# One Trainium2 core, a transformer block: query-key products two feature groups at a time, one evacuation for three modulation rows, a new order of work

## The chip, the cores and the metric

The kernel runs on one core of a Trainium2 chip. The metric is device time in microseconds (us) of one execution. A core has five engines, each with its own queue that it works through in order: TensorE (PE in the profile; PEld is its weight load), VectorE (DVE), ScalarE (ACT), GpSimd (POOL) and SyncE (SP), which here only issues transfers (DMA). SBUF is the on-chip memory of 128 partitions, PSUM the memory that TensorE writes.

## The reference

The block is modulated by a vector `c`: its SiLU, multiplied by `w_mod`, gives six rows of 512 (`sa`, `ca`, `ga`, `sb`, `cb`, `gb`). Part A is attention over 2048 positions with 32 heads of 16 features, in which each query sees 8 keys, at distances 0, 2, ... 14. Part B is a token mixer: an MLP along the positions.

```python
    def _A_ref(x, wqkv, wo):            # H = 32, Dh = 16, W, dil = 8, 2
        ...
        logits = jnp.einsum('bhsd,bhswd->bhsw', q, kg) * scale
        logits = jnp.where(mask[None, None, :, :], logits, -1000000000.0)
        attn = _softmax(logits, axis=-1)
        o = jnp.einsum('bhsw,bhswd->bhsd', attn, vg)
        return (lambda x, *d: x.transpose(*d))(o, 0, 2, 1, 3).reshape(B, S, D) @ wo
    def _B_ref(x, w1, b1, w2, b2):
        h = _layernorm(x, axis=-1)
        u = _gelu(jnp.einsum('bsd,sf->bdf', h, w1) + b1)
        y = jnp.einsum('bdf,fs->bds', u, w2) + b2
        return (lambda x, *d: x.transpose(*d))(y, 0, 2, 1)
    ...
    h = _layernorm(x, axis=-1) * (1 + ca) + sa
    x = x + ga * _A_ref(h, A_wqkv, A_wo)
    h = _layernorm(x, axis=-1) * (1 + cb) + sb
    x = x + gb * _B_ref(h, B_w1, B_b1, B_w2, B_b2)
```

## The kernel before

The 2048 positions are 16 tiles of 128. They go through part A in five chunks of 2, 4, 4, 4 and 2 tiles (`SIZES`), so a chunk has C = 256 or 512 columns. Part B follows once the second layernorm of the tiles it needs is done.

**Order.** The program is a graph of some 780 named operations. `ORDER` (from line 192) is a table of their names, written out in full, that sets the place of each in its engine's queue; a letter behind the name picks the engine where there are several (`:a` ACT, `:d` DVE, `:p` POOL, `:s` SP), `:q` asks for a TensorE product in four pieces of 32 output partitions, `:n` leaves an accumulation into PSUM to the evacuating engine, and `fill:n` puts n idle products on TensorE. `schedule` (line 86) walks the table and hands out buffers of three rings: six PSUM tiles (`ps`), four product buffers (`big`) and five value buffers (`vd`). Nearly all instructions are recorded by one helper, so they carry line 143; they are told apart by tiles and shapes.

**Part A of chunk c, by the names of the table.** `ln1s`, `ln1v`, `rstd1`, `nb1` are the statistics of the first layernorm and `n1_t` its output for tile t. `xt` transposes two tiles by DMA (chunks 2 to 4; `tr` does it on TensorE for 0 and 1). `qkv{c}_{t}{j}` multiplies by the weights (t = 0 query, 1 key, 2 value; j the feature group), and `ev{c}_{t}{j}` evacuates the result. The 16 features of a head are held as 4 groups of 4, so `qk{c}_{d}` (line 761) multiplies, for group d, the queries with the 8 shifted keys: 8 x C products a partition into one `big` buffer. `red{c}_{d}` sums four partitions of it on TensorE into the PSUM tile `psL`, over the four groups. Then come `max` (DVE, from `psL`), `sub` (TensorE), `exp` (ACT), `esum` (TensorE; DVE in chunk 4), `rcp` (ACT) and `smB` (DVE), whose result `lsb` is spread over partitions by four transfers `a2_{c}_{j}`. Four transfers `vd{c}_{q}` bring shifted values, `pv{c}_{q}` (DVE) multiplies them with the weights into a `big` buffer, `pvacc` (TensorE) sums, `oev` (ACT) evacuates, `wo{t}` (TensorE) multiplies by `wo`, and `x1_{t}` adds into `xx`.

**Second layernorm and part B.** `ln2q`, `rstd2`, `nb2`, `n2_t` (layernorm), `aff` (line 903: times 1 + cb, plus sb, on a group of tiles), `ln3s`, `ln3v`, `rstd3`, `nb3`, `h3_t` (part B's own layernorm). `mlp1_{i}_{f}_{s}` is the first product for feature tile f and position tiles from s on; it comes in two or three sweeps i, whose partial sums `park` and `padd` keep in `gT`. The pieces whose names end in `_10` with i = 1 and f from 7 on need all of `h3` from tile 10 to 15. Then `gelu`, `mlp2` for each of 16 output tiles, `fin` (two DVE operations) and the store `st_out`.

**Modulation rows.** `build_mod_rows` (line 588) makes four rows: `modrow0` (ga), and `modrow1` (sb, cb, gb together) on TensorE; `mrows0` on ACT and `mrows1` on DVE bring them to SBUF. `mrows1` is two DVE instructions, a copy of three rows, and a second read of the middle one with 1 added. `st_row` and `ld_row` then spread the rows over all partitions through DRAM.

`halo_k3` copies the last 16 key columns of chunk 2 to the start of the key buffer that chunk 3 reuses; it may run only when chunk 2's `qk` are done.

Of the kernel before, what the change touches and what calls it, by code (L numbers as in the profile page):

```python
# [8 lines left out]
ALU = mybir.AluOpType  # L9
# [33 lines left out]
class _Graph:  # L43
# [42 lines left out]
    def schedule(self):  # L86
# [4 lines left out]
        for pos, token in enumerate(ORDER.split()):  # L91
# [111 lines left out]
wsc1_1:p wsc0_2:p n1_7:p n1_9:p wsc1_2:p n1_6:p smB0 qk1_2 wsc2_3:a qkv1_22:q red1_0 qkv1_21:q modrow1 wsc2_0:a
a2_0_1:a ev1_22:a ev1_21:a ln1s15 nb1_3 red1_1 qkv1_23:q red1_2 red1_3 mrows1 max1 xt6 xt8 qkv1_20:q ev1_23:a wsc2_1:a
ev1_20:a qkv2_00:q qkv2_10:q vd0_2 vd0_3 vd0_1 ld_wo2 vd0_0 st_row0 a2_0_2:s a2_0_3:s a2_0_0:s ld_wo3 ld_row0 ld_wo0
n1_11:p n1_10:p pv0_1 pv0_2 pv0_3 pv0_0 sub1:q ev2_00:a biascols_cp:a exp1 ev2_10:a qkv2_03:q pvacc0_2 qkv2_11:q
fill:6:q qkv2_13:q esum1:q pvacc0_3 n1_12:a n1_13:a ev2_13:a ev2_03:a oev0_2:a pvacc0_0 pvacc0_1 rcp1 rstd1_4 oev0_0:a
qk2_0 woq_s smB1 qk2_3 qkv2_01:q qkv2_12:q qkv2_02:q ev2_11:a ev2_01:a a2_1_1:a ev2_12:a ev2_02:a qk2_1 qk2_2 wo1:q
x1_1:a wo0:q x1_0:a ln2q1 xt10 xt12 red2_0 qkv2_23:q qkv3_22:q qkv3_12:q vd1_0 st_row1 vd1_2 ev2_23:a ln2q0 rstd2_0
nb1_4 nb2_0 qkv2_21:q ev2_21:a red2_1 a2_1_2:s a2_1_0:s a2_1_3:s vd1_1 ld_row1 vd1_3 n1_14:p pv1_2 qkv3_13:q red2_2  # L210
red2_3 max2 qkv2_22:q n1_15:a ev3_13:a n2_1:a ev3_12:a ev2_22:a n2_0:a halo_v2:p qkv2_20:q sub2:q ev2_20:a exp2
pvacc1_2 qkv3_10:q halo_v3:a oev1_2:a ev3_10:a qkv3_02:q qkv3_20:q pv1_1 qkv3_01:q pvacc1_1 esum2:q ev3_02:a ev3_20:a
# [5 lines left out]
max3 sub3:q pvacc2_3 exp3 esum3:q oev2_3:a rstd3_0 pv2_2 nb2_4 pvacc2_2 qkv4_10:q rcp3 n2_5:a oev2_2:a n2_4:a pv2_1
pvacc2_1 fill:4:q oev2_1:a wo6:q wo7:q wo8:q wo9:q ev4_00:a smB3 n2_3:p vd3_3 ld_w1_0_896 vd3_1 vd3_0 a2_3_2:s a2_3_3:s
a2_3_0:s a2_3_1:s vd3_2 ld_w2_1 aff2 nb3_0 aff4 h3_1:p h3_0:p halo_v4:p ln3s3:a ln3s2:d ln3s4:d ln3v3 ln3v2 ln3v4  # L220
ln3s5:a ln3v5 pv3_1 x1_8:a x1_7:a x1_6:a rstd3_2 ev4_10:a h3_3 h3_2 mlp1_0_1_0 mlp1_0_2_0 mlp1_0_5_0:q mlp1_0_3_0:q
pvacc3_1 rstd3_4 nb3_4 x1_9:a pv3_2 pv3_3 pv3_0 h3_4:a h3_5:a oev3_1:a mlp1_0_2_2:q mlp1_0_1_2:q mlp1_0_0_0:q
mlp1_0_0_2:q mlp1_0_3_2:q mlp1_0_0_4:q mlp1_0_5_2:q mlp1_0_5_4:q mlp1_0_3_4:q mlp1_0_1_4:q pvacc3_2 mlp1_0_2_4:q ln2q9
ln2q6 park0_0:a park0_1:a ln2q7 park0_2:a oev3_2:a qk4_0 qk4_2 mlp1_0_4_0:q mlp1_0_4_2:q pvacc3_3 mlp1_0_6_0:q ln2q8
oev3_3:a mlp1_0_6_2:q pvacc3_0 mlp1_0_6_4:q mlp1_0_4_4:q oev3_0:a mlp1_0_7_0:q wo13:qn red4_0 rstd2_6 nb2_6 park0_3:a
qk4_1 x1_13:d n2_9:a n2_6:a park0_4:a wo12:q n2_8:p ld_w1_0_1152 ld_w1_0_1408 vd4_1 ld_w2_3 vd4_2 vd4_0 vd4_3 n2_7:d
# [27 lines left out]
def kernel(  # L254
# [823 lines left out]
```

## Time and profile before

| what | value |
|---|---|
| median of 3 runs | 198.86 us (198.62 to 199.24) |
| profiled execution, its own time | 198.75 us |
| its span, first to last instruction | 197.0 us |
| PE busy | 185.8 us (94%) |
| DVE busy | 157.3 us (80%) |
| ACT busy | 127.1 us (64%) |
| POOL busy | 22.8 us (12%) |
| granted clock of TensorE | 0.997 |

The span leaves out 1.75 us that the time of the same execution has around it. The shares are means over stages: DVE, for instance, is busy in nine tenths or more of each fortieth of the span from 15 to 128 us, and much less in the last third. Rows of the profile give start, duration, engine, line, operation, output<-input and, where there is one, the idle time ahead of it with what ended it, in brackets.

### The profile page before, as it was taken

What the parts mean: (1) busy time and instruction counts of PE and PEld (TensorE: products, weight loads), DVE (VectorE), ACT (ScalarE), POOL (GpSimd) and SP (SyncE); (2) the same over time, 40 slices, a digit from 0 to 9 for tenths busy, and PEclk for the clock granted to TensorE, in tenths of its full rate; (3) what the DMA queues carried; (4) which work ended last, traced back from release to release, by engine and by line L of the source; (5) the groups of instructions that cost most, each with busy time, mean ns of one, the idle gap of its engine ahead of it and who ended that gap; (6) DMA issues with size and microseconds to landing.
All of it is one profiled execution on the core that took longest, in us unless ns stands there. A gap on an engine that the chain in (4) does not pass through costs nothing.

```text
span 197.0 us, 5568 instructions
## 1 busy us (share of the span) xinstructions
PE 185.8 (94%) x2331; PEld 99.5 (50%) x2343; DVE 157.3 (80%) x222; ACT 127.1 (64%) x304; POOL 22.8 (12%) x46
## 2 busy tenths in 40 slices
PE   3999999999999996899999999999999999999993
PEld 1476656565465674435554454444444444444462
DVE  2789999999999999999999999977550207864693
ACT  4799999898999999999997899735660000000000
POOL 4184003000500001130031000500000000000000
PEclk9999999999999999999999999999999999999998
DMA  5999695888997449180497494588999200144113
GB/s 156 357 355 341 226 259 137 101 201 253 302 303 268 149 144 322 34 218 14 136 245 208 91 255 97 157 273 177 290 348 339 61 0 15 38 130 99 53 53 107
DMA packets 53893, 36.02 MB, mean 183 GB/s; under 512 B 24428, under 2 KB 50668, under 8 KB 53868
## 3 DMA queue, kind: packets, MB, share of 16 engines
q1 hardware_dynamic: 52772, 35.27, 64.2%
q10 hardware_dynamic: 1096, 0.39, 0.8%
q8 instruction: 18, 0.29, 0.6%
q14 instruction: 7, 0.06, 0.1%
HBM read 22.55 MB, written 2.10 MB: 125 GB/s over the span
## 4 chain that ended last, share of the span: by engine, by line
PE 63%; DVE 21%; issue 5%; DMA 4%; SPq 3%; ACT 2%; DVEq 0%; ACTq 0%
PE psS L143 61%; DVE big L143 14%; DMA xx<-in_A_x_dram 4%; DVE h L143 4%; SPq L143 3%; PE psL L143 2%; DVE lsb L143 1%; DVE st L143 1%; ACT xx L143 1%; ACT junk L143 1%; DVE m L143 1%; DVE nb L143 0%; ACT k_f L143 0%; DVE woq L143 0%; ACT rs L143 0%
## 5 line engine op out<-in xcount | busy, mean ns | idle before, releaser
L143 PEld LDWEIGHTS <-wst 128*128 128x128 bf16 (+1 forms) x578 | 35.6, 101 | 32.7 <-issue 2.8
L143 PE MATMUL psS<-h,wst 128*32 128x512 bf16 (+1 forms) x350 | 50.1, 379 | 0.4 <-issue 0.2
L143 DVE TENSOR_TENSOR big<-a2sb,vD 128x4096 bf16<-128x4096 bf16 (+1 forms) x20 | 36.4, 1857 | 0.1
L143 DVE TENSOR_TENSOR big<-q_sb,k_f 128x4096 bf16<-128x4096 bf16 (+1 forms) x20 | 36.3, 1857 | 0.0
L143 PE MATMUL psS<-hT,w_qkv 128*32 128x512 bf16 (+1 forms) x576 | 29.0, 344 | 0.0
L143 DVE SCALAR_TENSOR_TENSOR h<-psS,bcol,rows_bc 128x512 f32<-128x512 f32 (+2 forms) x17 | 12.1, 709 | 21.2 <-PE psS L143 21.0
L143 PEld LDWEIGHTS <-w_qkv 128*32 128x32 bf16 (+1 forms) x618 | 21.2, 107 | 13.9
L143 PE MATMUL psS<-gT,big 128*128 128x512 bf16 x111 | 24.8, 379 | 0.1
L143 POOL TENSOR_SCALAR h<-xx,rs,nb 128x512 bf16<-128x512 bf16 x11 | 11.5, 1047 | 94.3 <-DVE nb L143 40.6
L143 PEld LDWEIGHTS <-big 128*128 128x128 bf16 x144 | 12.1, 98 | 13.8 <-DMA big<-in_w_mod_dram 0.5
L143 PE MATMUL psS<-woq,o_sb 128*32 128x512 bf16 (+1 forms) x220 | 16.7, 379 | 0.3 <-ACT o_sb L143 0.3
L143 ACT ACTIVATE gT<-psS,bcol 128x512 bf16<-128x512 f32 x14 | 8.9, 685 | 8.6 <-DVE psS L143 8.6
L143 DVE TENSOR_TENSOR psS<-psS,gT 128x512 f32<-128x512 f32 x14 | 9.4, 697 | 5.5 <-PE psS L143 5.5
L143 DVE TENSOR_TENSOR h<-h,xx 128x512 bf16<-128x512 f32 (+2 forms) x17 | 11.1, 652 | 2.6 <-DMA out_dram<-h 2.1
L143 PE MATMUL psS<-hT,wst 128*32 128x512 bf16 (+2 forms) x134 | 11.8, 355 | 0.2
L143 DVE TENSOR_TENSOR h<-h,rows_bc 128x1024 bf16<-128x1024 bf16 (+2 forms) x16 | 11.5, 718 | 0.5
L143 ACT ACTIVATE v_sb<-psS,qvb 128x512 bf16<-128x512 f32 (+1 forms) x20 | 11.1, 599 | 0.7 <-PE psS L143 0.7
L143 DVE BATCH_NORM_STATS2 st<-xx 128x6 f32<-128x512 bf16 x12 | 7.9, 681 | 4.5 <-DMA xx<-in_A_x_dram 4.5
L143 PEld LDWEIGHTS <-group 128*32 128x32 bf16 x288 | 7.7, 96 | 7.3 <-DVE big L143 1.7
L143 PE MATMUL psS<-big,group 128*32 128x512 bf16 (+1 forms) x160 | 9.9, 338 | 1.1 <-DVE big L143 0.8
L143 ACT ACTIVATE q_sb<-psS,qvb 128x512 bf16<-128x512 f32 (+1 forms) x18 | 10.6, 614 | 0.4 <-PE psS L143 0.3
L143 PEld LDWEIGHTS <-o_sb 128*32 128x32 bf16 (+1 forms) x220 | 7.0, 97 | 7.1 <-ACT o_sb L143 0.8
(106 smaller groups left out, 249.3 us busy)
## 6 DMA issues: line engine op xcount, KB each, us to landing
vD<-v_sb SPq DMA_DIRECT2D x12, 524.5 KB, 5.1
big<-in_B_w_dram SPq DMA_DIRECT2D x4, 896.0 KB, 8.3
vD<-v_sb SPq DMA_DIRECT2D x8, 268.5 KB, 2.5
wst<-in_B_w_dram SPq DMA_DIRECT2D x3, 640.0 KB, 4.4
out_dram<-h SPq DMA_DIRECT2D x15, 128.0 KB, 1.8
wst<-in_B_w_dram SPq DMA_DIRECT2D x2, 800.0 KB, 5.4
xx<-in_A_x_dram SPq DMA_DIRECT2D x6, 256.0 KB, 7.2
gT<-in_w_mod_dram SPq DMA_DIRECT2D x4, 384.0 KB, 7.6
```

The lines of the kernel that those rows point to most:

```text
L143: r = fn(*a, **k)
```

## The change

Three things are changed, and `ORDER` is written anew behind its first five lines.

1. `qk{c}_{d}` does two groups in one instruction (d = 0 and 2), for all chunks (`QKP`). The four `big` buffers become two tiles with two halves each; a product pair of a 4-tile chunk takes both halves of a tile (`size` 2 in `schedule`), one of a 2-tile chunk takes one half. The output is laid out group, shift, position, and `red` picks its quarter of the positions with a stride. `red` still sums one group at a time.
2. `mrows1` is one copy that may go to ACT; the 1 is added on TensorE, by four small products of a column of ones with the identity at the end of `modrow1`.
3. `aff` is split in two operations, `afm` (times) and `afs` (plus), each with its own place in the table. The instructions are the same.

```diff
-                o.alloc.i = min((freed[p][k], k) for k in range(self.pools[p]) if held[p][k] is None)[1]
-                held[p][o.alloc.i] = o.alloc
+                z = o.alloc.size
+                o.alloc.i = min((max(freed[p][k:k + z]), k) for k in range(0, self.pools[p] - z + 1, z)
+                                if held[p][k:k + z] == [None] * z)[1]
+                held[p][o.alloc.i:o.alloc.i + z] = [o.alloc] * z
...
-    big_r = ring(NBIG, [P, NW * CM], BF, "big")
+    big_t = ring(NBIG // 2, [P, 2, NW * CM], BF, "big")
+    big_r = [big_t[i // 2][:, i % 2, :] for i in range(NBIG)]
...
-                                             rhs=w_[:, kt, dt_ * P:(dt_ + 1) * P], start=(kt == 0), stop=(kt == KT - 1),
+                                             rhs=w_[:, kt, dt_ * P:(dt_ + 1) * P], start=(kt == 0),
+                                             stop=(kt == KT - 1 and (r0, r) != (1, 1)),
                                              tile_position=(0, 32 * dt_))
+                    if (r0, r) == (1, 1):
+                        for dt_ in range(KT):
+                            nc.tensor.matmul(ps(s_)[32 * dt_:32 * dt_ + 32, r * P:(r + 1) * P],
+                                             lhsT=ones[:, 0:1].to_broadcast([P, 32]), rhs=ident[:], start=False, stop=True,
+                                             tile_position=(0, 32 * dt_))
...
-                def f_cp(rows=rows, src_=src_):
-                    nc.vector.tensor_copy(rows, src_())
-                    nc.vector.tensor_scalar_add(rows[:, 1, :], src_()[:, 1, :], 1.0)
-                add("dve", 0.8, f_cp, writes=[("mrows", b_)], frees=s_, name=f"mrows{b_}")
+            copy2(rows, src_, nr * P, False, [], [("mrows", b_)], f"mrows{b_}", frees=s_)
...
-        for dlo in range(4):
-            s_ = _Slot("big")
+        NQ = 2 if ch in QKP else 1
+        for d0 in range(0, 4, NQ):
+            s_ = _Slot("big", NQ * C // CM or 1)
...
-            def f(dlo=dlo, prod=prod):
-                qv = _ap(q_sb[:, dlo, 0:1], [[0, NW], [SB, 4], [1, SB]])
-                kv = _ap(k_c[:, dlo, PAD:PAD + 1], [[-DIL, NW], [SB, 4], [1, SB]])
-                nc.vector.tensor_tensor(_ap(prod()[:, 0, 0, 0:1], [[SB, NW], [NW * SB, 4], [1, SB]]), qv, kv,
-                                        op=ALU.mult)
+                return _ap(big_t[s_.i // 2][:, s_.i % 2, 0:1], [[NW * C, NQ], [C, NW], [1, C]])
+
+            def f(d0=d0, prod=prod):
+                qv = _ap(q_sb[:, d0, 0:1], [[C, NQ], [0, NW], [1, C]])
+                k0, k1 = k_c[:, 0, PAD:PAD + 1], k_c[:, 1, PAD:PAD + 1]
+                kv = _ap(k_c[:, d0, PAD:PAD + 1], [[k1.offset - k0.offset, NQ], [-DIL, NW], [1, C]])
+                nc.vector.tensor_tensor(prod(), qv, kv, op=ALU.mult)
...
-                                         rhs=prod()[:, jj, hf * WPM:(hf + 1) * WPM, :], start=(dlo == 0),
...
+                                             rhs=pr[:, hf * WPM:(hf + 1) * WPM, jj * SB:(jj + 1) * SB], start=(dlo == 0),
```

The first place of the new order that matters is DVE's queue around the softmax of chunk 0 and the products of chunk 1. `m` is the output of `max`, `lsb` that of `smB`, `big<-q_sb,k_f` is a `qk` and `big<-a2sb,vD` a `pv`. Before:

```order
L143 TENSOR_TENSOR big_86<-q_sb_80,k_f 128x8x4x128
L143 TENSOR_REDUCE m_94<-psL 128x64
L143 TENSOR_TENSOR big_87<-q_sb_80,k_f 128x8x4x128
L143 TENSOR_TENSOR big_85<-q_sb_80,k_f 128x8x4x128
L143 TENSOR_TENSOR lsb_88<-lsb_88,rb 128x512
L143 TENSOR_TENSOR big_84<-q_sb_80,k_f 128x8x4x128
L143 SCALAR_TENSOR_TENSOR nb_130<-mv_127,rs_129 128x4
L143 CAST mrows<-psS_65 128x384
L143 TENSOR_SCALAR mrows<-psS_65 128x128
L143 TENSOR_REDUCE m_94<-psL 128x128
```

And now:

```order
L146 TENSOR_TENSOR v_sb_82<-psS_67,qvb 128x2x256
L146 SCALAR_TENSOR_TENSOR nb_129<-mv_126,rs_128 128x4
L146 TENSOR_SCALAR w_qkv_73<-h_102,a1col 128x512
L146 TENSOR_REDUCE m_92<-psL 128x64
L146 TENSOR_TENSOR big_84<-q_sb_80,k_f 128x8192
L146 TENSOR_TENSOR lsb_86<-lsb_86,rb 128x512
L146 TENSOR_TENSOR big_85<-q_sb_80,k_f 128x8192
L146 TENSOR_TENSOR big_84<-a2sb_88,vD_95 128x2048
L146 TENSOR_TENSOR big_84<-a2sb_88,vD_97 128x2048
L146 TENSOR_REDUCE m_92<-psL 128x128
```

No product of chunk 1 stands ahead of chunk 0's `max` any more; a value evacuation (`ev0_20`) and a scaling of weights (`wsc2_2`) that were ACT's stand there instead, the two instructions of `mrows1` are gone from DVE, and two `pv` of chunk 0 stand ahead of chunk 1's `max`.

The second place is DVE's queue at the last layernorms of part A, from `x1_14` (`xx<-psS,xx`) on; `st` and `mv` are statistics, `h_76` is `h3`, `gT<-psS,gT` a `park`. Before, the last rows:

```order
L143 TENSOR_TENSOR h_103<-h_103,rows_bc 128x512 x2
L143 SCALAR_TENSOR_TENSOR nb_140<-mv_137,rs_139 128x2
L143 BN_STATS st_2_136<-h_103 128x6
L143 BN_AGGR mv_137<-st_2_136 128x2
L143 TENSOR_TENSOR gT<-psS_68,gT 128x512
L143 SCALAR_TENSOR_TENSOR nb_140<-mv_137,rs_139 128x1 x2
L143 TENSOR_TENSOR gT<-psS_63,gT 128x512
```

And now:

```order
L146 TENSOR_TENSOR h_101<-h_101,rows_bc 128x512
L146 SCALAR_TENSOR_TENSOR mv_136<-mv_136,st_2_135 128x1
L146 BN_STATS st_2_135<-h_101 128x6
L146 BN_AGGR mv_136<-st_2_135 128x2
L146 SCALAR_TENSOR_TENSOR nb_139<-mv_136,rs_138 128x1
L146 TENSOR_TENSOR gT<-psS_67,gT 128x512
L146 SCALAR_TENSOR_TENSOR nb_139<-mv_136,rs_138 128x1
L146 TENSOR_SCALAR h_76<-h_101,rs_138,nb_139 128x512
```

The statistics of tile 14 are now taken on ACT, a `park` stands between the last two `nb3`, and the norm of tile 15 (`h3_15`), which was ACT's, is the last of them on DVE. On ACT `h3_11` now comes after `rstd3_15`; it stood three places ahead of it.

More of the change, by code (lines that the diff above doesn't have):

```diff
@@ L203 @@
[L203 to L212, printed above, removed]
@@ L218 @@
[L218 to L226, printed above, removed]
-qk4_3 wo11:q red4_1 red4_2 red4_3 ln2q13 x1_12:a ln2q12 park0_5:a x1_11:a rstd2_12 aff6 ln3s7:a mlp1_0_9_0 mlp1_0_9_2
@@ new lines @@
+oev0_2:a fill:1:q qkv2_03 oev0_0:a wo0:q wo1:q rstd1_4 ev2_02:a vd1_0 a2_1_3:s a2_1_2:s a2_1_0:s vd1_2 st_row1 vd1_3
+a2_1_1:s ld_row1 ev2_03:a ev2_12:a wsc2_0:a qk2_2 x1_1:a x1_0:a halo_v2:a ln2q1 ln2q0 rstd2_0 nb2_0 qkv3_10 red2_0
+red2_1 qkv3_12:q qkv2_20:q qkv2_22:q ev2_20:a ev2_22:a ev3_10:a red2_2 red2_3 nb1_4 ev3_12:a n2_1:a halo_k3:p n2_0:p
+pv1_2 qkv3_11 qkv3_00 ev3_00:a n1_14:a n1_15:a max2 qkv2_21:q ev2_21:a sub2:q qkv3_01:q qkv3_13:q pvacc1_2 ev3_11:a
+exp2 ev3_01:a oev1_2:a qkv2_23 esum2:q fill:14:q afm0 pv1_3 pv1_0 pvacc1_3 pvacc1_0 afs0 rcp2 ev2_23:a ln3s1 ev3_13:a
@@ L347 @@
     epscol = T([P, 1], F32, "epscol")
+    ones = T([P, 1], BF, "ones")
     a1col = T([P, KT], F32, "a1col")
```

125 lines of the change are left out of this document (72 added, 53 removed).

## The prediction

> **What bounds the kernel now.** First the busy time by stretches, cut where the work changes: attention, attention with part B starting at its end, the last layernorms, part B alone.
>
> ```profile
> core 0: us, PE busy (x) PEld busy (x) DVE busy (x) ACT busy (x) POOL busy (x), PEclk, DMA share, GB/s
> 16.50:50.00 33.50, 33.44 (x723) 19.62 (x727) 33.00 (x32) 31.45 (x75) 2.07 (x4) 1.00 0.80 215
> 50.00:88.70 38.70, 35.19 (x771) 20.93 (x764) 38.47 (x33) 37.61 (x93) 6.10 (x6) 1.00 0.76 216
> 88.70:128.40 39.70, 39.44 (x405) 19.46 (x408) 38.57 (x71) 35.76 (x93) 5.53 (x6) 1.00 0.59 150
> 128.40:193.60 65.20, 64.88 (x324) 30.99 (x328) 35.89 (x55) 10.15 (x15) 0.00 (x0) 1.00 0.52 144
> ```
>
> Three engines are full at once. Of the 111.9 us from 16.5 to 128.4, DVE is idle for 1.9; PE's idle time lies almost all in the second stretch. From 128.4 to the end PE alone counts, with full clock. Then the waits: whom DVE waits for, and where PE waits in the second stretch.
>
> ```profile
> DVE m L143 <- PE psL L143: 0.3, 1, 0.3
> DVE xx L143 <- PE psS L143: 0.2, 1, 0.2
> ```
>
> ```profile
> 76.20 0.62 PE L143 MATMUL psL<-m,nident 128*32 128x512 bf16 x8 [1.04 <-DVE m L143]
> 78.05 0.63 PE L143 MATMUL psS<-lsb,ident 128*32 128x128 bf16 x32 [0.80 <-ACT lsb L143]
> 80.68 0.61 PE L143 MATMUL psS<-big,group 128*32 128x512 bf16 x8 [0.69 <-DVE big L143]
> ```
>
> Between 17 and 118 us DVE runs through its list nearly without a stop and PE waits for it. So the time is: start to 17 us, DVE's list up to the last `h3`, and from there PE's remaining work. That last part is fixed: by the table, 301 passes of 512 columns stand behind the first piece that needs all of `h3`, before and after alike, and they are the 65.2 us of the fourth row. The change can move the end only by moving the moment of the last `h3`.
>
> ```profile
> 119.34 0.69 DVE L143 TENSOR_TENSOR xx<-psS,xx 128x512 bf16<-128x512 f32 x1 [0.25 <-PE psS L143]
> 125.88 2.40 POOL L143 TENSOR_SCALAR h<-h,rs,nb 128x512 bf16<-128x512 bf16 x3 [1.09 <-DVE nb L143]
> 127.56 0.81 ACT L143 ACTIVATE h<-h,nb,rs 128x512 bf16<-128x512 bf16 x1 [0.34 <-DVE nb L143]
> ```
>
> `h3_14` ends on POOL at 128.28, `h3_15` on ACT at 128.37: that moment is 128.4 now.
>
> **The change part by part.** *Merged products.*
>
> ```profile
> L143 DVE TENSOR_TENSOR big<-q_sb,k_f 128x4096 bf16<-128x4096 bf16 x12 | 26.9, 2282 | 0.0
> L143 DVE TENSOR_TENSOR big<-q_sb,k_f 128x2048 bf16<-128x2048 bf16 x8 | 9.4, 1219 | 0.0
> 61.65 8.89 DVE L143 TENSOR_TENSOR big<-q_sb,k_f 128x4096 bf16<-128x4096 bf16 x4
> 17.46 4.63 DVE L143 TENSOR_TENSOR big<-q_sb,k_f 128x2048 bf16<-128x2048 bf16 x4
> ```
>
> Twice the elements cost 2282 against 1219 ns, so 1063 ns per 2048 and a fixed part of 156 ns. Back to back the instructions overlap: four take 8.89, from start to start (8.89 - 2.28) / 3 = 2.203 us, and (4.63 - 1.22) / 3 = 1.137 for the small ones. Of that 2.203, 2.126 are elements, so 0.077 is what an instruction costs here; 0.074 for a small one. Ten go away: 0.74 us, 0.60 of it before chunk 3's softmax. The bounds are these 0.74 and 10 x 0.156 = 1.56; I take the first, since these products stand back to back. [...]
>
> The reductions read with a stride now. The `qkv` products of chunk 1 read a packed `hT`, those of chunks 2 and 3 one in pieces of 128:
>
> ```profile
> L143 PE MATMUL psS<-hT,w_qkv 128*32 128x512 bf16 x384 | 23.1, 379 | 0.0
> L143 PE MATMUL psS<-hT,wst 128*32 128x512 bf16 x96 | 6.1, 381 | 0.0
> ```
>
> No difference, so nothing is charged for pieces of 128; pieces of 64 (chunks 0 and 4) are taken as equal.
>
> *Modulation rows, and work moved to DVE.*
>
> ```profile
> L143 DVE CAST mrows<-psS 128x384 bf16<-128x384 f32 x1 | 0.5, 549 | 0.0
> L143 DVE TENSOR_SCALAR mrows<-psS 128x128 bf16<-128x128 f32 x1 | 0.3, 290 | 0.0
> L143 ACT ACTIVATE mrows<-psS 128x128 bf16<-128x128 f32 x1 | 0.3, 259 | 0.0
> 16.67 0.69 DVE L143 TENSOR_TENSOR q_sb<-psS,qvb 128x512 bf16<-128x512 f32 x1
> 108.99 1.06 DVE L143 TENSOR_SCALAR h<-h,rs,nb 128x512 bf16<-128x512 bf16 x3
> 127.40 3.07 DVE L143 TENSOR_TENSOR gT<-psS,gT 128x512 bf16<-128x512 f32 x5
> ```
>
> DVE loses 0.84 us; ACT gains a copy between 0.26 (128 columns) and 0.6 us, which its slack takes. But in the same stretch `ev0_20` (0.60 start to start, as the 16.67 row) and `wsc2_2` ((1.06 - 0.41) / 2 = 0.33) come to DVE. Up to chunk 3's `smB`: -0.60 - 0.84 + 0.93 = -0.5 us. Against it stands a new wait:
>
> ```profile
> 24.22 0.23 PE L143 MATMUL psL<-mask,ident 32*32 32x128 bf16 x1
> 24.48 0.69 DVE L143 TENSOR_REDUCE m<-psL 128x64 bf16<-128x512 f32 x1
> ```
>
> Before, a product of chunk 1 covered the time until the mask was in. Now DVE has done both products at 17.46 + 2 x 2.20 = 21.9, and with `ev0_20`, `wsc2_2` and two small ones is at 23.0; PE has one group less ahead of the mask, which then ends at 24.45 - 0.87 = 23.6. That is 0.5 us of DVE standing, with chunk 1's products queued behind, and later work shifted equally. So `smB3`, at 80.54 now, comes within 0.2 us of that.
>
> *From there to the last `h3`.* Coming to DVE: `n2_5`, `n2_8`, `n2_10`, `h3_5`, `h3_10`, `h3_15` (6 x 0.33), and a `park` ahead of the last `nb3` ((3.07 - 0.66) / 4 = 0.60). Leaving: `n2_7`, `n2_12`, `n2_14` (-0.99) and two merges (-0.15, counted above). The `x1` and `ln3s` exchanges cancel. Sum +1.4. Against it, the 1.0 us from DVE's last `nb3` (127.4) to the end of `h3_15` on ACT goes, and the 0.25 us wait of `x1_14`, since `wo14` now is ready in time: +0.2. PE, two passes shorter from chunk 3's first `pvacc` on (180 for 182), would be there at 127.7, so DVE's list decides. Those 0.7 us to spare also have to hide `h3_6`, which DVE now makes third of three norms (0.66 us behind the first) and which the first pass on PE wants. `h3_11` on ACT, behind `rstd3_15`, ends about 128.4, as `h3_15` does. The pieces take the tiles in order, so the second pass waits for it.
>
> *The rest.* Four small products of ones (0.06 us by 219 ns each in four strips) and fillers, 0.4 us longer in sum, lie where PE waits for DVE; if that cover went, 0.5 us. The split `aff` is the same two instructions. From DVE's side +0.2, from the merges' uncertain size down to -0.8: I put the sum at -0.05 us against the execution's 198.75 (span 197.0 and 1.75 around it): **198.7 us**. That execution lies 0.11 under the median of 198.86.
>
> **Rivals.** *Faster: 197.9.* Each merge saves the full 0.156 us, 0.82 more than I counted, and the new waits are covered; for it speaks the duration row, against it the starts. [...]
>
> *Slower by POOL: 199.7.*
>
> ```profile
> 49.96 2.76 POOL L143 TENSOR_SCALAR h<-xx,rs,nb 128x512 bf16<-128x512 bf16 x1 [16.09 <-ACT v_sb L143]
> 49.79 2.28 DVE L143 TENSOR_TENSOR big<-a2sb,vD 128x4096 bf16<-128x4096 bf16 x1
> 104.87 0.77 POOL L143 TENSOR_SCALAR h<-xx,rs,nb 128x512 bf16<-128x512 bf16 x1 [4.66 <-DVE nb L143]
> ```
>
> A POOL norm takes 0.77 us alone and 2.76 beside a product: it gets through when the product is over. Now `halo_k3` and then `n2_0` are POOL's, free only when chunk 2's last `qk` ends, with `pv1_2` on DVE right after. `n2_0` then runs under `max2` (1.2 us) and is done just before `afm0` wants it. If it needs two gaps, `afm0` and everything behind it on DVE lose about 1.0: 199.7. It decides from 0.2 us late on. [...]
>
> *Slower by a transfer: 200.2.*
>
> ```profile
> 22.96 2.96 SPq L143 DMA_TRANSPOSE hT<-h  x2
> hT<-h SPq DMA_TRANSPOSE x5, 3.1
> 33.89 1.91 PE L143 MATMUL psS<-hT,w_qkv 128*32 128x512 bf16 x32
> ```
>
> Chunk 2's first product is used at 33.89 now; in the new order it stands about 4.5 us earlier on PE (29.4), while SP reaches its second transpose at about 23.6, behind `vd0_3`. With 1.5 us of issue and 3.1 to land it is there by 28.2. If weights still in flight make it 3 us later, PE stands 1.5 us and `red1`, `max1` and DVE with it: 200.2.
>
> *It does not do what it says.* The merged product falls out of its rate: at half of it, 36 us of products double, past 230 us. Operands and types are those of now, so this is nearly excluded.
>
> **Chances.** No change 0.38; faster 0.33; POOL 0.14; transfer 0.13; not as said 0.02. With 0.3% (0.6 us, about what a measurement of this kernel tells from no change) as the line: faster 0.33, same 0.38, slower 0.29. The likeliest case alone spans 198.1 to 199.3; the range reaches to both sides' cases: 197.3 to 200.4.
>
> **What would show it.** Right: merged products at about 4.41 us, start to start 4.33; DVE idle for some 0.5 us ahead of `max0`; `smB3` near 80.5; the last `h3` within 0.6 us of 128.4; 65 us of PE behind it. Wrong: a wait of DVE for POOL's `h` ahead of `afm0`; PE idle at 29 us for `hT`; or a `smB3` a microsecond earlier, which would mean that the merges free more than their spacing.

## The result, and the profile after

The changed kernel takes 199.74 us (median of 11 executions, 198.98 to 200.37) against 198.92 (198.46 to 199.52) for the kernel before on the same chip: ratio 1.0045, 95% interval 1.0029 to 1.006. It is slower by 0.8 to 0.9 us. Two repeats of the whole comparison gave 1.0049 (1.0023 to 1.0074) and 1.0033 (1.0007 to 1.0058). The profiled execution took 200.16 us, span 198.4, against 198.75 and 197.0.

Here are rows of DVE's timeline from the first query-key product to chunk 1's softmax, after the change (start, duration, operation, idle time before it and what ended that):

```profile
18.05 4.49 DVE L146 TENSOR_TENSOR big<-q_sb,k_f 128x4096 bf16<-128x4096 bf16 x2
23.50 0.16 DVE L146 SCALAR_TENSOR_TENSOR nb<-mv,rs 128x4 f32<-128x4 f32 x1 [0.23 <-ACT rs L146]
24.03 0.69 DVE L146 TENSOR_REDUCE m<-psL 128x64 bf16<-128x512 f32 x1
24.64 4.42 DVE L146 TENSOR_TENSOR big<-q_sb,k_f 128x8192 bf16<-128x8192 bf16 x1
28.97 0.42 DVE L146 TENSOR_TENSOR lsb<-lsb,rb 128x512 bf16<-128x512 bf16 x1
29.30 4.42 DVE L146 TENSOR_TENSOR big<-q_sb,k_f 128x8192 bf16<-128x8192 bf16 x1
35.34 2.36 DVE L146 TENSOR_TENSOR big<-a2sb,vD 128x2048 bf16<-128x2048 bf16 x2 [1.62 <-DMA a2sb<-lsb]
37.62 1.22 DVE L146 TENSOR_REDUCE m<-psL 128x128 bf16<-128x1024 f32 x1
```

The merged products do what was said: 4.42 us each, 4.33 from start to the next start. Then DVE has nothing to do for 1.62 us, at 33.7: `pv0_3`, chunk 0's first value product, waits for chunk 0's weights (`a2sb`), which four transfers carry away from `lsb` once `smB0` (28.97) has scaled them. The kernel before shows no such wait:

```profile
29.49 0.42 DVE L143 TENSOR_TENSOR lsb<-lsb,rb 128x512 bf16<-128x512 bf16 x1
29.83 2.29 DVE L143 TENSOR_TENSOR big<-q_sb,k_f 128x4096 bf16<-128x4096 bf16 x1
34.55 1.23 DVE L143 TENSOR_TENSOR big<-a2sb,vD 128x2048 bf16<-128x2048 bf16 x1
```

There `smB0`'s end and the first value product lie 4.64 us apart (29.91 to 34.55), filled by one product, `mrows1` and `max1`. Now one merged product stands between, 4.33 us (29.39 to 33.72). The chain of work that ended last goes through this place after the change; here are pieces of it there, and how it goes on (start, duration, what):

```profile
28.43 1.24 SPq L146
29.77 0.67 SPq L146
30.48 0.66 SPq L146
31.19 3.46 DMA a2sb<-lsb
36.49 1.22 DVE big L146
37.70 1.15 DVE m L146
38.89 0.64 PE psL L146 x8
84.10 8.67 PE psS L146 x122
```

SP, still issuing a value transfer until 29.67, sends off three of the four transfers one behind the other. The last leaves 1.80 us behind the end of `smB0`, lands 3.46 us later (34.65), and DVE starts 0.69 us after that: 5.95 us in all, where DVE's list covers 4.33. The difference is the wait. It goes on to `max1` and so to PE, which stood ahead of `sub1`:

```profile
38.89 0.61 PE L146 MATMUL psL<-m,nident 128*32 128x512 bf16 x8 [1.27 <-DVE m L146]
```

From 84.1 on the chain is PE's to the end. Before, it was DVE's for most of the way from 41 to 84 us, but from 88.67 on it was PE's as well:

```profile
88.67 10.66 PE psS L143 x192
```

At the two marks of the prediction:

```profile
82.51 0.69 DVE L146 TENSOR_TENSOR lsb<-lsb,rb 128x1024 bf16<-128x1024 bf16 x1 [0.34 <-ACT rb L146]
129.40 0.41 DVE L146 TENSOR_SCALAR h<-h,rs,nb 128x512 bf16<-128x512 bf16 x1
129.80:195.00 65.20, 64.94 (x412) 30.91 (x416) 35.65 (x55) 9.93 (x15) 0.00 (x0) 1.00 0.48 137
```

`smB3` comes at 82.5 (80.5 before), the last `h3` ends at 129.8 (128.4), and behind it stand the same 65 us of PE.

### The profile page after: what moved, and what is told of

Read it like the earlier page. It is cut to its first block, busy times and chain, and to the rows that moved or that the text cites. A ratio compares the mean times of both kernels' runs of the same rounds, so it can differ in the third digit from the quotient of the medians.

```text
span 198.4 us, 5551 instructions
## 1 busy us (share of the span) xinstructions
PE 188.4 (95%) x2325; PEld 96.5 (49%) x2337; DVE 156.8 (79%) x215; ACT 124.9 (63%) x299; POOL 25.0 (13%) x47
## 4 chain that ended last, share of the span: by engine, by line
PE 77%; ACT 9%; DMA 3%; SPq 3%; DVE 3%; issue 2%; POOL 0%; ACTq 0%; DVEq 0%
PE psS L146 74%; SPq L146 3%; PE psL L146 3%; DMA a2sb<-lsb 2%; ACT v_sb L146 2%; ACT lsb L146 1%; DMA c_t<-in_c_dram 1%; ACT o_sb L146 1%; ACT junk L146 1%; DVE h L146 1%; ACT h L146 1%; ACT q_sb L146 1%; DVE big L146 1%; DVE m L146 1%; ACT hT L146 1%
## 5 line engine op out<-in xcount | busy, mean ns | idle before, releaser
L146 PEld LDWEIGHTS <-wst 128*32 128x32 bf16 (+1 forms) x824 | 36.1, 100 | 32.5 <-issue 2.5
L146 PE MATMUL psS<-h,wst 128*32 128x512 bf16 (+1 forms) x588 | 50.7, 379 | 0.2
L146 DVE TENSOR_TENSOR big<-q_sb,k_f 128x8192 bf16<-128x8192 bf16 (+1 forms) x10 | 35.3, 3565 | 0.0
L146 PE MATMUL psS<-hT,w_qkv 128*32 128x512 bf16 (+3 forms) x384 | 30.0, 348 | 0.0
L146 PEld LDWEIGHTS <-w_qkv 128*32 128x32 bf16 (+1 forms) x426 | 19.3, 109 | 17.5 <-issue 5.4
L146 PE MATMUL psS<-woq,o_sb 128*32 128x512 bf16 (+1 forms) x156 | 15.5, 380 | 0.6 <-issue 0.3
L146 POOL TENSOR_SCALAR h<-xx,rs,nb 128x512 bf16<-128x512 bf16 x10 | 8.1, 816 | 61.6 <-DVE nb L146 25.9
L146 DVE TENSOR_TENSOR h<-h,rows_bc 128x1024 bf16<-128x1024 bf16 (+2 forms) x16 | 10.8, 683 | 0.1
L146 ACT ACTIVATE h<-xx,nb,rs 128x512 bf16<-128x512 bf16 x13 | 10.3, 807 | 0.5 <-DVE nb L146 0.5
L146 ACT ACTIVATE junk<-xx,sums 128x512 bf16<-128x512 bf16 x14 | 10.0, 716 | 0.1
```

The lines of the kernel that those rows point to most:

```text
L146: r = fn(*a, **k)
```

## The experiments

An edit is given in the words of the order table; where nothing else is said, it is made to the changed kernel.

**Which of the four transfers goes first.** Three edits, meant to bring the first product its own weights sooner or later:

```diff
 e1 and its repeat
-a2_0_0:s a2_0_1:s a2_0_3:s st_row0
+a2_0_3:s a2_0_0:s a2_0_1:s st_row0
 e7
-smB0 a2_0_2:a      ...      a2_0_0:s a2_0_1:s a2_0_3:s
+smB0 a2_0_3:a      ...      a2_0_0:s a2_0_1:s a2_0_2:s
 e8, in the kernel before
-a2_0_1:a      ...      a2_0_2:s a2_0_3:s a2_0_0:s
+a2_0_2:a      ...      a2_0_3:s a2_0_0:s a2_0_1:s
```

> Edit: of chunk 0's three weight transfers on SP, a2_0_3, which the first value product (pv0_3) needs, is issued first in place of third. Theory 1 (late weights: the 1.62 us in which DVE waits for it at 33.7 us is what the change lost, and it is passed on to the end): its issue moves from 31.2 to 29.8 us, the wait falls from 1.62 to 0.3 us or less, everything behind on DVE comes 1.3 us earlier, and the time falls by 0.9 to 1.3 us, to about 198.6 (0.998 to 1.000 of the kernel before). Theory 2 (TensorE's own order sets the end, DVE's wait is filled up again before the last h3): the wait goes, the time stays at 199.7 (1.0045). Theory 3 (the transfer lands when what is in flight lets it, not by its place): the wait stays above 1.2 us and the time stays.

> Edit: ACT issues a2_0_3 (for the first value product) and SP a2_0_2 (for the last) in place of the other way round, as the kernel before does it, where the first product's weights go over ACT's own queue. In four profiles so far the span is the start of pv0_3 plus 163.1 to 163.3 us, so what counts is when pv0_3 starts. Theory 1 (the first product waits for what stands ahead of its weights on SP's queue): pv0_3 starts with no wait, 33.1 to 33.7 us into the span, in nearly all runs; span about 196.5, time 198.0 to 198.6 (0.996 to 0.999 of the kernel before), runs within 0.6 us of each other. Theory 3 (the landing is set by what is in flight on the 16 DMA engines, whichever queue issues): the wait stays over 1 us in most runs, time 199.5 to 200.1 (1.003 to 1.006).

> The kernel before with one thing of the change done to it: the weights of its first value product (pv0_1) are issued last on SP and not on ACT (a2_0_2 goes over ACT). Theory 1: a2_0_1 is issued at 31.2 us and lands near 34.7; DVE, there at 34.5, waits 0.3 to 1.2 us, time 199.2 to 199.9 (1.001 to 1.005 of the kernel before), runs more apart than its own. Rival (the kernel before has enough slack there): no wait, 198.9 (1.000).

Measured: e1 1.0029 (1.0000 to 1.0058), e7 1.0041 (1.0014 to 1.0068), e8 1.0009 (0.9986 to 1.0032). None differs clearly from the kernel that it was made from, and the profile of e7 still waits 1.34 us. The reason is in the code: a value product reads all four parts.

```
reads=[("a2sb", ba, jj) for jj in range(4)] + [("vD", ch, dq)]
```

The expectations took a part for each product. What starts `pv0_3` is the last of the four, whichever it is. So these runs changed nothing, and they serve as repeats. e1 was profiled twice:

> The kernel with a2_0_3 first on SP once more, for a second profile: its times lay between 198.2 and 200.6, and the profiled one was the shortest. Theory 1: where the time is above 199.5, the profile shows DVE waiting for a2_0_3 (1 to 2 us) and an issue on SP ahead of it that takes longer than 0.7 us; the span is the start of pv0_3 plus 163.2 us. Rival: no such wait in a run above 199.5, and the time is lost elsewhere.

The first execution, of 198.19 us, and the second, of 200.21:

```profile
28.81 4.42 DVE L146 TENSOR_TENSOR big<-q_sb,k_f 128x8192 bf16<-128x8192 bf16 x1
33.24 2.36 DVE L146 TENSOR_TENSOR big<-a2sb,vD 128x2048 bf16<-128x2048 bf16 x2
```

```profile
28.59 4.42 DVE L146 TENSOR_TENSOR big<-q_sb,k_f 128x8192 bf16<-128x8192 bf16 x1
35.05 2.36 DVE L146 TENSOR_TENSOR big<-a2sb,vD 128x2048 bf16<-128x2048 bf16 x2 [2.03 <-DMA a2sb<-lsb]
```

The same program, once without the wait and once with 2.03 us of it: the spans, 196.5 and 198.5 us, lie 2.0 us apart. The one without took 0.56 us less than the profiled execution of the kernel before (198.19 to 198.75); it is the shortest of e1's twelve, whose median is 200.08. How long the wait is differs by execution, with the issue and with the landing of the last transfers. Here are the last two on SP, in the first and in the second execution (issue time, first and last start; time from issue to landing):

```profile
L146 SPq DMA_DIRECT2D a2sb<-lsb x2: 616/618/620, 29.6 to 30.3; - x2
DMA to landing us min/median/max: 2.2/2.5/2.7
```

```profile
L146 SPq DMA_DIRECT2D a2sb<-lsb x2: 612/622/633, 30.3 to 31.0; - x2
DMA to landing us min/median/max: 2.4/2.9/3.3
```

In the first the last transfer leaves 1.4 us behind the end of `smB0` (28.90) and lands 2.2 later; in the second it leaves 2.4 behind (28.61) and lands 3.3 later. So about half of the difference is SP, which came late: its two transposes ahead took 2.14 and 1.82 us to issue there, 1.35 and 1.32 in the first.

**The changed kernel again**, in two later groups:

> The changed kernel itself once more, beside the others of this group. Theories 1 and 3 alike: 199.2 to 200.4, ratio 1.003 to 1.006; in its profile the span is the start of pv0_3 plus 163.1 us (within 0.3), whatever that start is. If the span is not tied to that start, the late weights are not what sets the time.

> The changed kernel itself, third time, as the mark for this group: 199.4 to 200.2, ratio 1.003 to 1.006 by either theory.

The profiles so far whose DVE order is that of the changed kernel, and two of the order before (us; the first product's start differs by execution as well, as the two of e1 show):

| profile | first product | wait for weights | `pv0` | span | span less first product |
|---|---|---|---|---|---|
| before | 17.46 | 0 | 34.55 | 197.0 | 179.5 |
| before, e8 | 17.82 | 0.39 | 35.15 | 197.7 | 179.9 |
| changed, e1 | 17.55 | 0 | 33.24 | 196.5 | 179.0 |
| changed, third | 17.86 | 0.80 | 34.34 | 197.8 | 179.9 |
| changed, second | 17.55 | 1.04 | 34.26 | 197.9 | 180.4 |
| changed, e7 | 18.07 | 1.34 | 35.09 | 198.2 | 180.1 |
| changed, first | 18.05 | 1.62 | 35.34 | 198.4 | 180.4 |
| changed, e1 again | 17.26 | 2.03 | 35.05 | 198.5 | 181.2 |

Over the six of the changed order the last column grows with the wait, from 179.0 without one to 181.2 with 2.03 us; 179.0 plus the wait meets each within 0.4 us. Counted from `pv0` the rest of the span is 163.1 to 163.6 us, so the tie that the expectations took from the first profiles (163.1, within 0.3) is looser than they say. By these profiles the order itself is some 0.5 us shorter than the one before; the wait, 1.1 us on average over these six, is more.

There is a second difference, and it is in every profile of the changed order. Busy times from the first query-key product to the end, before, after, and in e1's first execution (stretch, its length, then PE first):

```profile
17.46:197.03 179.57, 172.02 (x2207) 90.63 (x2210) 145.37 (x185) 114.04 (x271) 13.20 (x14) 1.00 0.63 172
18.05:198.43 180.38, 174.31 (x2201) 87.77 (x2200) 144.68 (x179) 111.68 (x265) 16.39 (x16) 1.00 0.62 170
17.55:196.47 178.92, 174.23 (x2201) 87.77 (x2202) 144.97 (x178) 111.62 (x265) 16.04 (x15) 1.00 0.63 172
```

Between the last two, with and without the wait, it is the time without PE that differs (6.1 and 4.7 us). Against the kernel before, where that is 7.6, PE is busy 2.2 to 2.3 us longer, though the products recorded there come to nearly the same work (770 and 772 passes of 512 columns). The new order does more of the first MLP products in four pieces (lines of the whole profile, before and after):

```profile
L143 PE MATMUL psS<-h,wst 128*128 128x512 bf16 x174 | 39.2, 379 | 0.4 <-issue 0.2
L143 PE MATMUL psS<-h,wst 128*32 128x512 bf16 x176 | 10.9, 379 | 0.0
L146 PE MATMUL psS<-h,wst 128*32 128x512 bf16 x488 | 28.6, 379 | 0.1
L146 PE MATMUL psS<-h,wst 128*128 128x512 bf16 x100 | 22.2, 379 | 0.1
```

In the changed kernel a pass costs 0.234 us in pieces (28.6 / 122) and 0.222 whole (22.2 / 100); for the 78 passes more in pieces that would be an estimated 0.9 us. No run undid TensorE's part of the new order, so what the longer busy time costs, and whether it comes of this, stays open.

**The last transfer later still.**

```diff
-a2_0_0:s a2_0_1:s a2_0_3:s st_row0 ld_wo3 vd0_2 ld_row0
+a2_0_0:s a2_0_1:s st_row0 ld_wo3 vd0_2 a2_0_3:s ld_row0
```

> Edit: a2_0_3 is issued behind st_row0, ld_wo3 and vd0_2, so about 1.7 us later than in the changed kernel. Theory 1: DVE's wait ahead of pv0_3 grows from 1.6 to about 3.3 us and the time by 1.2 to 1.7 us, to about 201.2 (1.010 to 1.013 of the kernel before). Theory 2: the wait grows and the time by less than 0.5 us (1.004 to 1.007). Theory 3: the wait stays near 1.6 us, the time near 199.7.

Measured 204.2 us, 1.0269 (1.0236 to 1.0301): the wait grew by 2.3 us, to 3.93, and the time by 4.5, more than any theory said. The rows of PE's wait and of the stretches behind it (PE busy first, the granted clock third from the end):

```profile
41.51 1.04 PE L146 MATMUL psL<-m,nident 128*32 128x512 bf16 x8 [3.59 <-DVE m L146]
40.00:45.00 5.00, 3.49 (x20) 1.51 (x19) 4.86 (x5) 1.99 (x3) 0.00 (x0) 0.50 0.57 140
45.00:50.00 5.00, 5.00 (x87) 2.33 (x84) 3.13 (x2) 3.89 (x11) 0.00 (x0) 0.82 0.18 45
```

PE stood 3.59 us, and its granted clock was 0.50 from 40 to 45 us and 0.82 from 45 to 50. DVE then stood again, 1.06 us for chunk 1's `rb` and 0.95 us for PE. In the changed kernel PE stood 1.27 us and kept clock 1.00 from 37 to 50 us. What part of the 4.5 us the lower clock is, no run shows. In these runs, then, a wait of the changed kernel's size is passed on at about its length (2.03 us of wait and 2.0 us of span in e1's two executions), and the growth by 2.3 us at twice that.

**The merges undone** for chunks 1 to 3, alone and later with the smaller wait of the next edit:

```diff
-    QKP=(0, 1, 2, 3, 4, ),
+    QKP=(0, 4, ),
-qk1_0 ... qk1_2 ... qk2_0 ... qk2_2 ... qk3_0 ... qk3_2
+qk1_0 qk1_1 ... qk1_2 qk1_3 ... qk2_0 qk2_1 ... qk2_2 qk2_3 ... qk3_0 qk3_1 ... qk3_2 qk3_3
```

> Edit: the query-key products of chunks 1, 2 and 3 are undone, two instructions for each merged one (six more instructions on DVE, in the same places); chunks 0 and 4 stay merged. Prediction's price: 0.074 us for each, so 0.45 us of DVE in all. Theory 1: the two of chunk 1 stand ahead of DVE's wait and vanish in it (the wait falls to about 1.5), the four of chunks 2 and 3 cost 0.3 us: about 200.0 (1.006). Theory 2 (DVE is not what sets the end): no loss, or a gain where TensorE gets the first half of a product 2.2 us earlier: 199.7 or less (1.0045 or below). Rival of the fixed price (0.156 us each): +0.6 to 0.9 us, 200.5 (1.008).

> Edit: two of the four transfers on ACT, and the query-key products of chunks 1 to 3 undone (six more instructions on VectorE, 0.45 us at the prediction's 0.074 us each). Prediction's theory (VectorE's list sets the end, the merges are worth their instructions): 0.3 to 0.5 us slower than the merged one of this group (0.0015 to 0.0025 in the ratio). Rival (TensorE, full from 16 us on, or the transfers set the end, and what VectorE saves ends in a wait): within 0.2 us of the merged one, or faster.

Measured 1.0033 (1.0006 to 1.006) and 1.0014 (0.9999 to 1.003), beside 1.0033 to 1.0049 and 1.0012 for the merged ones. Six instructions more on DVE cost nothing that can be measured: the medians of e16 and of its merged twin (e15, below) are 199.17 and 199.10 us. Where chunk 3's share goes, in e4:

```profile
63.27 8.89 DVE L146 TENSOR_TENSOR big<-q_sb,k_f 128x4096 bf16<-128x4096 bf16 x4
82.27 0.69 DVE L146 TENSOR_TENSOR lsb<-lsb,rb 128x1024 bf16<-128x1024 bf16 x1
```

Four products take 8.89 us here, two merged ones 8.75, so a merge is worth its 0.07. But the merged kernel's `smB3` waited 0.34 us for ACT's `rb` (the row at 82.51), and this one doesn't wait: there DVE came earlier and stood. That is one pair of profiles; in the third profile of the changed kernel `smB3` has no such wait.

**Two evacuations back to ACT.**

```diff
-ev0_20:d      ...      wsc2_2:d
+ev0_20:a      ...      wsc2_2:a
```

> Edit: the value evacuation ev0_20 and the weight scaling wsc2_2, which the change gave to DVE ahead of chunk 0's mask reduction, go back to ACT: 0.9 us less on DVE before 24 us. Theory 1: what DVE saves there is lost in the wait for a2_0_3, whose issue hangs on SP's queue and not on DVE: the wait ahead of pv0_3 grows by what is saved (to 1.6 to 2.5 us), pv0_3 starts within 0.4 us of 35.3, and the time stays at 199.7, or is up to 0.5 us longer by ACT's added work (1.004 to 1.007). Theory 2, or DVE's list as the bound with no absorbing wait: 0.6 to 0.9 us faster, 198.9 (1.000).

Measured 1.0057 (1.0034 to 1.008). The expected time came. The expected reason is not in the profile, but that is of an execution of 198.79 us, where the median is 200.13: `pv0_3` started at 33.97 without a wait, and DVE stood earlier, for ACT.

```profile
22.85 0.16 DVE L146 SCALAR_TENSOR_TENSOR nb<-mv,rs 128x4 f32<-128x4 f32 x1 [0.84 <-ACT rs L146]
29.05 0.46 DVE L146 TENSOR_TENSOR lsb<-lsb,rb 128x512 bf16<-128x512 bf16 x1 [0.65 <-ACT rb L146]
```

**The issue over two queues.**

```diff
-smB0 a2_0_2:a      ...      a2_0_0:s a2_0_1:s a2_0_3:s
+smB0 a2_0_2:a a2_0_3:a      ...      a2_0_0:s a2_0_1:s
```

> Every value product reads all four parts of the weights (the runs with a2_0_3 moved about among them changed nothing, since the last of the four still left at 30.3 to 31.2 us and landed 2.2 to 3.7 us later). Edit: ACT issues two of the four (a2_0_2, a2_0_3) and SP the other two, so the last issue starts at 30.2 to 30.5 us in place of 30.3 to 31.2. Theory 3a (the last of the four, counted from its issue, sets the start of pv0_3): it lands 0.5 to 0.7 us sooner, pv0_3 starts 34.3 on average in place of 34.9, the time falls by 0.5 us to 199.3 (1.002), with ACT's 0.7 us lying in its own waits. Theory 3b (landing is set by what is in flight until 34.4 us, whatever the issue): no change, 199.8 (1.0045).

> The changed kernel with two of chunk 0's four weight transfers issued by ACT, once more, beside the changed kernel itself and its variants. Theory 3a (these transfers leave one behind the other on SP, and the last of them starts pv0_3): 198.8 to 199.4 again, ratio 0.999 to 1.002, and 0.4 to 0.9 us under the changed kernel of this group. Rival (the 1.0001 [0.9972, 1.0029] of the first time was chance, since with the loads moved as well the same edit gave 1.0038): 1.003 to 1.005, as the changed kernel.

Measured 1.0001 (0.9972 to 1.0029) and, beside the changed kernel's 1.0033, 1.0012 (0.9998 to 1.0027); medians 199.15 and 199.10 us. In the second group the changed kernel's median was 199.55, so the edit brings back some 0.45 us. How, the profiles do not show. The first, of an execution of 200.53 us, has 1.33 us of idle ahead of `pv0_3`. It is put down to PE, but the last of the four transfers left at 31.1 and landed 3.5 us later, at 34.6, so DVE more likely stood for that. The second, of 198.64 us, waits 0.73 us, hardly less than the changed kernel's profile of its group (0.80). There the last transfer left 0.8 us behind the end of `smB0` and landed 3.6 us later; in the changed kernel it left 1.7 behind and landed 2.7 later. In this pair 0.9 us of issue is saved, and the last landing takes 0.9 us longer; in the first profile the last transfer left 1.6 us behind the end of `smB0` (29.51), so hardly any issue is saved there. Less the first product's start (18.25 and 17.43) the two spans, 198.8 and 196.9, fit the table: 180.6 with 1.33 us of idle, 179.5 with 0.73.

The same edit in the kernel before (`a2_0_2` to ACT):

> Edit: in the kernel before, ACT issues two of chunk 0's four weight transfers. If the weights are just in time there as well (its VectorE comes to the first value product 4.6 us behind the end of smB0, and one of its two profiles of that order waited 0.4 us), it gains 0 to 0.4 us: 198.4 to 198.8 (0.998 to 1.000). If it has slack, or ACT's 0.7 us lie on the path: 198.8 to 199.3 (1.000 to 1.003).

Measured 1.0012 (0.999 to 1.0035): no gain, as the second case has it. Its own order leaves enough time: in its profile the first value product starts at 34.27 without a wait.

**Less on SP ahead of the weights.**

```diff
 e10, and e11 with two transfers on ACT
-xt8 ld_wo2 ld_b1 vd0_0 vd0_1      ...      a2_0_3:s st_row0
+xt8 vd0_1      ...      a2_0_3:s ld_wo2 ld_b1 vd0_0 st_row0
 e12, and e13 with two transfers on ACT
-xt8 ld_wo2 ld_b1 vd0_0 vd0_1      ...      ld_row0 xt10 vd1_1
+xt8 vd0_0 vd0_1      ...      ld_row0 ld_wo2 xt10 ld_b1 vd1_1
```

> Edit: on SP the loads ld_wo2 and ld_b1 and the spread values vd0_0, which nothing needs before 38 us, are issued behind chunk 0's weights in place of ahead of them: about 1.75 us less of issuing ahead, and 0.4 MB less in flight when the weights are issued. Theory 3a: SP is free when smB0 ends, the last issue starts 0.1 to 0.9 us sooner: 199.2 (1.001 to 1.003). Theory 3b (what is in flight): the landing shortens to 2.0 to 2.5 us as well, pv0_3 starts with a wait under 0.5 us, time 198.2 to 198.8 (0.997 to 0.9995). If neither the wait nor the time changes, SP's list ahead of the weights isn't the cause.

> Both edits: two of the weight transfers on ACT, and ld_wo2, ld_b1 and vd0_0 behind them. If the wait ahead of pv0_3 is all that makes the changed kernel slower than the kernel before, it is gone here in most runs: pv0_3 starts at 33.2 to 33.8, the span is that plus 163.1 us, 196.3 to 196.9, and the time 198.0 to 198.6 (0.996 to 0.9985 of the kernel before). If the wait goes and the time stays above 199, the tie between the start of pv0_3 and the end, read off the profiles, is wrong.

> Edit: only ld_wo2 (issued behind ld_row0) and ld_b1 (behind xt10) leave SP's list ahead of chunk 0's weights; vd0_0 stays where it was, since moving it behind made two new waits (1.0 us for vd0_0, 0.8 us for the modulation row) in place of the one removed. Counted from the start of the first query-key product, pv0_3 started 15.65 us later without a wait and 16.7 to 17.8 us later with one (six profiles). Theory 3 (SP's list and what is in flight make the weights late): 15.7 to 16.3 us here, no new wait above 0.3 us, time 198.3 to 199.0 (0.997 to 1.001). If pv0_3 starts above 16.7 as before, SP's list is not it.

> Edit: the same, and two of the four weight transfers on ACT, which alone brought the changed kernel to 1.0001 [0.9972, 1.0029] of the kernel before. Theory 3: pv0_3 15.65 to 15.9 us behind the first product in most runs, time 198.0 to 198.6 (0.996 to 0.9985).

Measured 1.0048 (1.0021 to 1.0075), 1.0045 (1.0017 to 1.0072), 1.0031 (1.0013 to 1.005) and 1.0038 (1.0024 to 1.0052): the times missed. Yet in all four profiles `pv0_3` started 15.6 to 15.9 us behind the first product, with no wait of note. In e12 the last of the four left 1.4 us behind the end of `smB0`, as short as in e1's first execution, and `pv0_3` (33.40) did not wait for it. What e10 and e12 show in place of the wait:

```profile
38.91 1.23 DVE L146 TENSOR_TENSOR big<-a2sb,vD 128x2048 bf16<-128x2048 bf16 x1 [0.99 <-DMA vD<-v_sb]
40.97 1.23 DVE L146 TENSOR_TENSOR woq<-woq,rows_bc 128x2048 bf16<-128x2048 bf16 x1 [0.84 <-DMA rows_bc<-scratch]
```

```profile
33.40 2.35 DVE L146 TENSOR_TENSOR big<-a2sb,vD 128x2048 bf16<-128x2048 bf16 x2
50.92 2.29 DVE L146 TENSOR_TENSOR big<-a2sb,vD 128x4096 bf16<-128x4096 bf16 x1 [0.88 <-PE psS L146]
```

In e10 the values that were put behind came late themselves, and so did the modulation row behind them. In e12 a wait of 0.88 us stands ahead of chunk 1's first value product. In e13 it is 0.41 us for `woq`, whose load had been moved. In e11 (200.60 us) there is no wait of note on DVE: its first product began at 19.35, later than in any row of the table, so that execution lost its time ahead of all that was changed. Less the first product's start, the spans of e11, e12 and e13 are 179.6, 179.7 and 179.7 us, that of e10 180.6: none comes down to the 179.0 of e1. So the wait went, the time stayed, and the tie of e11's expectation is wrong: from `pv0` to the end these four took 163.8 to 165.0 us.

Chunk 1's wait has its own narrow cover in the changed kernel. In its first profile the last of chunk 1's four weight transfers left at 47.0 and landed 4.4 us later, at 51.4; chunk 1's first value product started at 51.59, with no wait and 0.2 us to spare. In e12 that transfer left 7.0 us behind the start of `smB1` in place of 4.8, since SP stood 3.92 us in the issue of a transpose (1.29 in the changed kernel).

**The weights sent off early.** As e12, and chunk 0's transfers take `lsb` before `smB0` scales it; `smB0` writes a tile that nothing reads.

```diff
-nc.vector.tensor_tensor(ee, ee, rb.unsqueeze(1)...
+nc.vector.tensor_tensor(ee if ch else dmy, ee, rb.unsqueeze(1)...
```

> Edit: chunk 0's weights are sent off before they are divided by their sum (the division, smB0, is still carried out, into a tile that nothing reads, so DVE's list is as long as before), so the transfers hang on exp0 at 27 us and not on smB0 at 29.4; the loads as in the run with ld_wo2 and ld_b1 later. What is left out: the scaling of chunk 0's softmax. This takes the wait away altogether. If the wait ahead of pv0_3 is all that the changed kernel lost, pv0_3 starts 15.6 to 15.7 us behind the first product in every run, the time is 197.9 to 198.5 (0.995 to 0.998 of the kernel before) and the runs lie closer together than the changed kernel's (198.5 to 201). If the time stays at or above 199, something else behind it holds the end.

Measured 1.0045 (1.0024 to 1.0067). That is a miss, and the most telling one:

```profile
33.21 2.35 DVE L146 TENSOR_TENSOR big<-a2sb,vD 128x2048 bf16<-128x2048 bf16 x2
36.11 1.23 DVE L146 TENSOR_REDUCE m<-psL 128x128 bf16<-128x1024 f32 x1 [0.54 <-PE psL L146]
41.97 0.69 DVE L146 TENSOR_TENSOR lsb<-lsb,rb 128x1024 bf16<-128x1024 bf16 x1 [1.24 <-ACT rb L146]
```

```profile
39.53 1.02 ACT L146 ACTIVATE lsb<-psL 128x1024 bf16<-128x1024 f32 x1 [1.96 <-PE psS L146]
```

The wait is gone, and 1.8 us go to waits in chunk 1's softmax, where ACT's `exp1` stood 1.96 us for PE. This execution took 200.90 us, where the median is 199.45, so a common one may lose less there. It also shows, small, what the prediction's transfer rival described: a transpose for chunk 2 landed 5.5 us after its issue, and PE stood 0.2 us for `hT` at 29.8. So the wait for the weights is what the changed kernel shows in its profiles, but not the only one that its order has: take it away by moving transfers, and the next stands 2 to 17 us behind it (at 35.6 in e14, at 50.0 in e12). The one in e12 was near in the changed kernel already, 0.2 us away, and the late transpose brought it out. Whether the others come of the moved transfers, or were hidden by the first wait, was not settled: there is one profile of each.

## Why the prediction went wrong

It said 198.7 and no change, with 0.29 for slower; 199.74 lies inside its range and on the slow side. By its steps:

*Merged products: size right, worth wrong.* 4.42 us and a start to start of 4.33 were forecast to 0.01, and a merge does save 0.07 us. The step "0.74 us" failed in taking that sum to the end: with six merges undone nothing was lost that could be measured. In the profiles DVE's saving ended in waits, for `a2sb` and, in one of them, for `rb`.

*The half microsecond ahead of `max0`* was 0.23 us, for `rs`. `max0` came 5.98 us behind the first product, forecast 6.1.

*"The time is: start to 17 us, DVE's list up to the last `h3`, and from there PE's remaining work"*: this is the step that failed. Along with DVE's list, the path from `smB0` over SP and the transfers to `pv0` has to be counted. The change took `mrows1` and `max1` out from ahead of the first value product and left 4.33 us there, where the first profile needs 5.95 and the six of the table up to 6.4 (4.33 plus the wait). The working priced DVE's instructions and one transfer (`xt8`), not this one: the term was put at nothing. Nor does PE wait for DVE all the way from 17 to 118 us, as the step has it: in the prediction's own rows PE is busy 33.44 of the 33.50 us of the first stretch and 39.44 of the 39.70 of the third. There is hardly any idle time there in which a delay of PE could vanish, and PE's work in the new order, busy 2.2 us longer, belonged in the sum, which has two passes, four small products and some fillers of it. DVE's list up to `smB3` came out as forecast: of `smB3`'s 1.97 us, 0.59 is the later start of that execution and 1.62 the wait (the remaining -0.24 is made of smaller gains and waits); in the execution without the wait (DVE's timeline of e1's first profile) `smB3` and the last `h3` come at

```profile
80.55 0.69 DVE L146 TENSOR_TENSOR lsb<-lsb,rb 128x1024 bf16<-128x1024 bf16 x1 [0.23 <-ACT rb L146]
127.44 0.41 DVE L146 TENSOR_SCALAR h<-h,rs,nb 128x512 bf16<-128x512 bf16 x1
```

with `smB3` as forecast (80.54 within 0.2).

*From `smB3` to the last `h3`: +0.2* was -0.5: 47.3 us (80.55 to 127.85, and 82.51 to 129.81) for 47.8 before. That is a term sized 0.7 too high, on the other side of the wait. Without the wait the time was 198.2, 0.6 below the execution before and near the rival at 197.9, but not by fuller merges: that it nearly met this rival would have been luck.

*PE's 65 us behind the last `h3`*: right, 65.2 less 0.3 idle. That DVE and not PE decides ahead of it was not borne out: the chain is PE's from 84 us after the change, and it was so from 88.67 before.

*Rivals.* POOL's didn't come: `n2_0` was done under `max2`, as the sum itself had it.

```profile
51.60 2.38 POOL L146 COPY k_f<-k_f 128x64 bf16<-128x64 bf16 x1 [27.02 <-DVE nb L146]
53.96 0.76 POOL L146 TENSOR_SCALAR h<-xx,rs,nb 128x512 bf16<-128x512 bf16 x1
54.93 0.68 DVE L146 TENSOR_TENSOR h<-h,rows_bc 128x1024 bf16<-128x1024 bf16 x1
```

The transfer rival was right in kind and near in price (1.5 us; the waits are 0 to 2.0) and wrong in place. In the first profile PE did not stand at 29 us for `hT`; where it did, it was for 0.4 us (the changed kernel's second), 0.4 (e1 again), 0.3 (e9) and 0.2 (e14). That 199.74 lies inside the range, near POOL's 199.7, is luck: neither that rival nor the sum has the wait that made it.

Shown: that between executions of the changed order the time follows the wait for the weights (two executions of one program, and the table), and that this path was missing from the sum. Not shown: that the wait is all that the change lost. With the wait gone, e10 to e14 were at 1.0031 to 1.0048 all the same, and PE's longer busy time was never tested. Undoing six merges cost nothing that could be measured. Likely, by the times 1.0001 and 1.0012 alone: that issuing one behind the other on SP is a part of the loss; the profiles of these two runs still wait. Open: the rest, and the second waits. No version tried was faster than the kernel before; the best, two transfers on ACT, is level with it.

## What to carry to other kernels

Before work is taken off an engine's list or moved behind, look for the transfer that starts and ends on that list: the instructions between the one that produces its data and the first that needs them are its cover, and it needs the issues ahead of the last transfer, that one's landing, and the start of the consumer: 1.80, 3.46 and 0.69 us in the first profile here. Read the consumer's code for all that it waits for: the order among four transfers is nothing if it needs all four. Where several engines are full, count the work of each before and after, not that of one. And one profile shows one draw of such a wait (0 and 2.03 us in e1's two): two executions of the same program that differ in it show what it is worth, and an edit that takes it away shows what stands behind it.

## What the runs showed of the hardware that was not expected

Transfers of 32 KB inside the core (`lsb` to `a2sb`) landed 2.0 us (chunk 4's on ACT in the changed kernel's first profile) to 4.5 us (one of chunk 0's in e9) after their issue; the last of chunk 0's four alone, in the six profiles of the table, 2.2 to 3.6. The merged product took 4.42 us in each of these. The two profiled executions of e1, which differ in the issue and the landing, took 198.19 and 200.21 us. And in e6 2.3 us of added wait cost 4.5 us: PE stood 3.59 us, and its granted clock was 0.50 from 40 to 45 us and 0.82 from 45 to 50.
